# Loading raw query weights in every block, pairing the softmax sums on VectorE, turning them one step earlier, and a steeper fill rate at the end

## The chip, the cores and the metric

The kernel runs on one core of a Trainium2 chip. The metric is the device time of one execution in microseconds (us). The core's engines have names of their own in the profile: PE is TensorE (its matmuls; PEld are its weight loads), DVE is VectorE, ACT is ScalarE, POOL is GpSimd, and SP is the engine whose queue issues all of this kernel's DMAs.

## The reference

Two independent parts are computed from different inputs and laid side by side in the output. Part A is attention with 32 query heads and one shared key and value head; part B is a two-dimensional Fourier mix by matrices, of which the real part is kept.

```python
def _A_ref(x, wq, wk, wv, wo):            # x 1 x 2048 x 1024, 32 heads of 32
    q = (x @ wq).reshape(B, S, H, Dh).transpose(0, 2, 1, 3)
    k = x @ wk
    v = x @ wv
    scores = jnp.einsum("bhqd,bkd->bhqk", q, k) * (Dh ** -0.5)
    p = softmax(scores, axis=-1)
    o = jnp.einsum("bhqk,bkd->bhqd", p, v)
    return o.transpose(0, 2, 1, 3).reshape(B, S, H * Dh) @ wo

def _B_ref(x, dft_seq_re, dft_seq_im, dft_hid_re, dft_hid_im):
    a = jnp.einsum("bsd,ed->bse", x, dft_hid_re)
    b = jnp.einsum("bsd,ed->bse", x, dft_hid_im)
    return jnp.einsum("ts,bse->bte", dft_seq_re, a) - jnp.einsum("ts,bse->bte", dft_seq_im, b)

return jnp.concatenate([a, b], axis=-1)   # 1 x 2048 x 2048, all float32
```

## The kernel before

**Two streams on TensorE.** One stream is attention. It is cut into 32 units (a block `b` of 512 query rows times a group `g` of four heads), and a unit into 32 steps. The other stream is "fill": all large products that are not attention, 5664 matmuls of 512 columns. These are the projections of keys, values and queries, both stages of part B (seven products each instead of eight) and the output projection. Each float32 operand of a fill product is split into a high part and a rest (`hi`, `lo`), and three matmuls (high times high, rest times high, high times rest) make one product.

**A step of attention.** `score_step(s)` writes a 128 x 1024 piece of the scores into a PSUM tile `pss` (two matmuls), DVE takes its row maximum into `nm`, and one step later ACT takes the exponential in place, whose row sums are accumulated (`row_sums`). After the 32 steps of a unit these maxima and sums give the softmax's shift and divisor. `LSE` is a table that says in which later step `e` of the next unit each of these small operations stands: `lse_1` (DVE), `lse_1b` (an exponential on ACT), `lse_1c` (a product on POOL), `lse_2` (DVE), `lse_3` (a PE matmul with the identity that turns `nm` by 90 degrees, "the turning matmul", and a DVE copy to `mt`), `lse_4` (DMAs that put `mt` into two rows of `qst`, the query tile, and the divisors to DRAM). Twelve steps after a unit's scores end (`LEAD`), `expo(n)` begins on it: the scores once more, transposed, in a PSUM tile `pst` (two matmuls), whose exponential ACT writes to `p`. `pst` has one buffer, so the next pair of its matmuls waits for ACT. Every eighth step `pv` multiplies eight tiles `p` with `v` (128 matmuls in a unit).

**The fill's place.** Instructions stand on each engine in the order in which the Python code issues them. `pos["fill"]` counts the fill matmuls issued. `START` = 144 of them come first; up to there the splits are cast on ACT and subtracted on DVE, from there on both are on POOL. Another 66 follow, then 44 steps of scores with seven fill matmuls each (`take(7)`), and then 1024 steps of the main loop, in which `level(n)` issues as many as bring the count to a goal that rises in a straight line. In the last 44 of these steps no scores of new units are left.

**The supply of the fill.** An `Item` is one operand tile of 128 x 512. A `Line` (`RL` for the right operands `r`, `ML` for the left ones `m`) takes its items through four stages (load by DMA, combine, high part, rest), each a fixed lead ahead of the item's due place, counted in fill matmuls: 52, 36, 27 and 21 for `ML`. A raw left tile has three buffers, a split one four. An item with `pre` instead fetches both finished parts from DRAM, in `fetch`. `store` issues a DMA nine fill matmuls after the call (`BEHIND`), so it does not hold up SP's queue.

**Query weights.** `q_group(b, g, xs)` makes the query projection of one unit: 24 fill matmuls, a left operand `wq` of two items. For block 0 the items are loaded raw, split, and both parts are stored to DRAM (`wq_d`); blocks 1 to 3 fetch the two parts. The 32 query groups are the fill matmuls 96 to 864.

Of the kernel before, what the change touches and what calls it, by code (L numbers as in the profile page):

```python
# [16 lines left out]
P = 128  # L17
# [5 lines left out]
NG = 8  # L23
NQ = 4
NC = 16
# [62 lines left out]
def tile_kernel(ctx: ExitStack, tc, xT, wq, wkv, wo, xbT, wT, cT, out):  # L88
    nc = tc.nc
    te = Ordered(tc, nc.tensor)  # L90
    act = Ordered(tc, nc.scalar)
    dve = Ordered(tc, nc.vector)
    gp = Ordered(tc, nc.gpsimd)
# [13 lines left out]
    wq_d = [[[dram.tile([P, 4, P], F32, name=f"wq_{g}_{q}_{a}") for a in range(2)] for q in range(2)] for g in range(NG)]  # L107
    xr_d = [dram.tile([P, 4, P], F32, name=f"xr_{k}") for k in range(8)]
    wr_d = [[dram.tile([P, W], F32, name=f"wr_{n}_{c}") for c in range(4)] for n in range(2)]
    u_d = {(n, k): [dram.tile([P, W], F32, name=f"{k}_{n}_{s}") for s in range(8)] for n in range(2) for k in ("t", "u2", "u3", "u4")}  # L110
# [306 lines left out]
        return Group(wkv_items, xs, kv_post(b), rows=2 * DH)  # L417

    ready = set()
    seen_w = set()  # L420

    def q_group(b, g, xs):
        if g in seen_w:
            left = [Item(None, pre=lambda q=q: wq_d[g][q]) for q in range(2)]
        else:
            seen_w.add(g)
            left = [Item([(lambda q=q: wq[g, :, q * 4:(q + 1) * 4, :], 1)], save=wq_d[g][q]) for q in range(2)]

        def post(ps):
            qh = op.tile([P, W], F32R, name="qh")  # L430
            ql = op.tile([P, W], F32R, name="ql", bufs=1)
            if pos["fill"] <= START:
# [152 lines left out]
    SU = 32  # L585
    LEAD = 12
    total = SU * len(units)
    qst, nm, ls, lse, pt, ov, rb, pend = ({} for _ in range(8))
    ends = []

    def open_unit(u):
        b, g = units[u]
        assert ("q", b, g) in ready
        q = qsp.tile([P, 4, W], F32R, name="qst")
        gp.memset(q[96:P].bitcast(F32), 0.0)
        for r, src in enumerate((qh_d, ql_d, qh_d)):
            move(sp, q[r * DH:(r + 1) * DH], src[b][g].rearrange("(h d) c -> d h c", d=DH))
        qst[u] = q
        nm[u] = sm.tile([P, 6, NC], F32, name="nm")
        ls[u] = sm.tile([P, 2, NC], F32, name="ls")  # L600

    def scores(s):
        u, r = divmod(s, SU)
# [9 lines left out]
    def row_sums(s):  # L613
        if s not in pend:
            return
        ps = pend.pop(s)
        u, r = divmod(s, SU)
        i, j = divmod(r, 2)
        act.activation(ps, ps, AF.Exp, bias=nm[u][:, j, i:i + 1], accum_out=ls[u][:, j, i:i + 1])

    def over(rows):
        return rows.rearrange("p a c -> p c a")

    def lse_1(u):
        z = nm[u]
        d = sm.tile([P, 2, NC], F32, name="md")
        dve.tensor_reduce(z[:, 2], over(z[:, :2]), axis=AX.X, op=ALU.min, negate=True)
        for j in range(2):
            dve.tensor_reduce(d[:, j], over(z[:, j::2 - j][:, :2]), axis=AX.X, op=ALU.add, negate=True)
        lse[u] = d  # L630

    def lse_1b(u):
        act.activation(lse[u], lse[u], AF.Exp)

    def lse_1c(u):
        gp.tensor_mul(lse[u], lse[u], ls[u])

    def lse_2(u):
        z, d = nm[u], lse[u]
        l = sm.tile([P, NC], F32, name="l")  # L640
        dve.tensor_reduce(z[:, 3].bitcast(F32R), over(z[:, :2]), axis=AX.X, op=ALU.min)
        dve.tensor_reduce(z[:, 4], over(z[:, 2:4]), axis=AX.X, op=ALU.add, negate=True)
        dve.tensor_reduce(l, over(d), axis=AX.X, op=ALU.add)
        dve.reciprocal(z[:, 5], l)

    def lse_3(u):
        aside()
        pm = bank("psb")
        te.transpose(pm[:3 * NC, :P], nm[u][:, 3:].rearrange("p a b -> p (a b)"), ident)
# [58 lines left out]
    def score_step(s):  # L708

        if s < total:  # L710
            u, r = divmod(s, SU)
            if r == SU - 6 and u + 1 < len(units):
                open_unit(u + 1)
            scores(s)
        row_sums(s - 1)
        u, e = divmod(s - SU, SU)
        if 0 <= u < len(units):
            for f in LSE.get(e, ()):
                f(u)
# [117 lines left out]
```

## Time and profile before

| | |
|---|---|
| median of three runs | 2813.98 us (2813.29 to 2816.73) |
| the profiled execution's own time | 2816.89 us |
| its span from first to last instruction | 2815.0 us |
| PE busy | 2776.0 us, 99% of the span |
| ACT, DVE, POOL busy | 2182.6, 1612.9, 1569.4 us |
| granted TensorE clock, mean | 0.997 |
| DMA | 480.84 MB, 171 GB/s over the span |

Rows of the profile that show an instruction name its output and input tiles without their buffer numbers, then the shape, then "xN" where N equal ones are merged. A time in brackets at the end is how long the engine was idle before it, with what ended the wait. "Windows" rows give for a stretch of time its length, each engine's busy time with the number of instructions, the granted clock as a share of full speed, the busy share of the 16 DMA engines, and GB/s. A matmul's listed duration overlaps with the next one's, so the distance between the starts of two matmuls is what one costs. Nearly every instruction of the kernel stands under line 66, a helper; tiles tell them apart.

### The profile page before, as it was taken

To read this page: it belongs to the slowest core of one execution; us is meant where nothing else is said; L and a number is where in the kernel's file an instruction comes from. 1 tells how busy PE (TensorE), PEld (TensorE's weight loads), DVE (VectorE), ACT (ScalarE), POOL (GpSimd) and SP (SyncE) were. 2 spreads that over 40 slices of the span, in tenths; PEclk is the share of its full clock that TensorE was granted. 3 is DMA by queue.
4 is the path that set the end of the run, shared out by engine and by line. 5 is a ranking of instruction groups with operands and counts; after the bars stand their busy time and mean duration, and the time that the engine had idled before them with its cause. 6 is when DMAs were issued, how large, how long until landed. Compare 5 with 4: busy or idle time off the path is not lost.

```text
span 2815.0 us, 40144 instructions
## 1 busy us (share of the span) xinstructions
PE 2776.0 (99%) x13904; PEld 1935.7 (69%) x13904; DVE 1612.9 (57%) x1800; ACT 2182.6 (78%) x3151; POOL 1569.4 (56%) x1558
## 2 busy tenths in 40 slices
PE   7999999999999999999999999989999999999999
PEld 5776676767667676767666767666767676766656
DVE  5766666666666665555555555545555555555411
ACT  4578887888878788888888888878888888888740
POOL 2422233665545448767785676887888875721110
PEclk9999999999999999999999999999999999999999
DMA  8865435675576555554463454564554642545345
GB/s 292 299 199 163 156 109 169 225 231 188 195 243 211 166 178 167 152 155 142 140 191 105 127 172 122 184 198 138 183 176 146 187 139 98 159 145 145 122 143 172
DMA packets 315723, 480.84 MB, mean 171 GB/s; under 512 B 33408, under 2 KB 98432, under 8 KB 315520
## 3 DMA queue, kind: packets, MB, share of 16 engines
q1 hardware_dynamic: 315520, 478.28, 54.3%
q8 instruction: 110, 1.80, 0.3%
q14 instruction: 93, 0.76, 0.1%
HBM read 364.12 MB, written 112.98 MB: 169 GB/s over the span
## 4 chain that ended last, share of the span: by engine, by line
PE 93%; DMA 2%; POOL 1%; issue 1%; DVE 1%; SPq 1%; ACT 1%; POOLq 0%; DVEq 0%; ACTq 0%
PE psb L66 59%; PE pss L66 18%; PE pst L66 17%; DMA r<-s 1%; DMA ql<-ql 1%; SPq L66 1%; POOL ml L66 0%; DMA r<-in_xT_dram 0%; DVE nm L66 0%; POOL mh L66 0%; POOL m L66 0%; DMA wq<-mh 0%; POOL rl L66 0%; POOL rh L66 0%; POOL y L66 0%
## 5 line engine op out<-in xcount | busy, mean ns | idle before, releaser
L66 DVE TENSOR_REDUCE nm<-pss 128x1 f32<-128x1024 f32 x1024 | 1252.2, 1223 | 611.7 <-PE pss L66 610.9
L66 ACT ACTIVATE p<-pst 128x1024 f32<-128x1024 f32 x1024 | 1052.0, 1027 | 481.0 <-PE pst L66 478.9
L66 ACT ACTIVATE pss<-pss,nm 128x1024 f32<-128x1024 f32 x1024 | 1112.7, 1087 | 72.7 <-DVE nm L66 71.6
L66 PE MATMUL psb<-rh,mh 128*128 128x512 f32 (+1 forms) x1852 | 732.0, 395 | 17.9 <-ACT rh L66 8.7
L66 PE MATMUL psb<-rh,ml 128*128 128x512 f32 (+1 forms) x1852 | 731.9, 395 | 1.4 <-POOL ml L66 1.4
L66 PE MATMUL psb<-rl,mh 128*128 128x512 f32 (+1 forms) x1852 | 730.1, 394 | 0.3 <-DVE rl L66 0.3
L66 PE MATMUL pst<-qst,kst 128*128 128x512 f32 x2048 | 654.3, 400 | 5.6 <-DMA qst<-mt 4.7
L66 PE MATMUL pss<-kst,qst 128*128 128x512 f32 x2048 | 655.8, 401 | 3.2 <-ACT pss L66 3.2
L66 PEld LDWEIGHTS pss<-kst,qst 128*128 128x128 f32 x2048 | 375.6, 188 | 185.3 <-issue 100.5
L66 PE MATMUL psb<-p,v 128*32 128x512 f32 x4096 | 466.6, 596 | 0.0
L66 PEld LDWEIGHTS pst<-qst,kst 128*128 128x128 f32 x2048 | 375.8, 188 | 116.6 <-ACT p L66 26.6
L66 PEld LDWEIGHTS psb<-rh,mh 128*128 128x128 f32 (+1 forms) x1852 | 347.6, 188 | 105.8 <-ACT rh L66 10.0
L66 PEld LDWEIGHTS psb<-rh,ml 128*128 128x128 f32 (+1 forms) x1852 | 347.8, 188 | 86.0 <-POOL ml L66 2.8
L66 PEld LDWEIGHTS psb<-rl,mh 128*128 128x128 f32 (+1 forms) x1852 | 347.4, 188 | 84.2 <-DVE rl L66 1.4
L66 POOL TENSOR_TENSOR ml<-m,mh 128x512 fp32r<-128x512 f32 x292 | 376.5, 1289 | 49.2 <-ACT mh L66 43.6
L66 PEld LDWEIGHTS psb<-p,v 128*32 128x32 f32 x4096 | 120.5, 110 | 276.3 <-issue 266.0
L66 POOL TENSOR_TENSOR r<-r,r 128x512 f32<-128x512 f32 x112 | 144.3, 1288 | 269.7 <-DMA r<-in_wT_dram 135.0
L66 POOL CAST rh<-r 128x512 fp32r<-128x512 f32 x214 | 131.2, 613 | 275.0 <-PE psb L66 110.1
L66 POOL TENSOR_TENSOR rl<-r,rh 128x512 fp32r<-128x512 f32 x214 | 276.0, 1290 | 5.5
L66 POOL TENSOR_TENSOR m<-m,m 128x512 f32<-128x512 f32 x192 | 247.6, 1290 | 24.4 <-DMA m<-in_xbT_dram 18.8
L66 DVE TENSOR_TENSOR ov<-ov,psb 128x512 f32<-128x512 f32 x96 | 66.0, 687 | 314.2 <-PE psb L66 314.2
L66 POOL CAST mh<-m 128x512 fp32r<-128x512 f32 x291 | 178.0, 612 | 91.4 <-PE psb L66 76.0
(69 smaller groups left out, 926.5 us busy)
## 6 DMA issues: line engine op xcount, KB each, us to landing
m<-in_cT_dram SPq DMA_DIRECT2D x384, 256.0 KB, 3.8
r<-s SPq DMA_DIRECT2D x192, 256.0 KB, 4.4
y<-y SPq DMA_DIRECT2D x96, 256.0 KB, 4.6
r<-in_wT_dram SPq DMA_DIRECT2D x80, 256.0 KB, 3.6
m<-in_xbT_dram SPq DMA_DIRECT2D x80, 256.0 KB, 4.2
y<-u SPq DMA_DIRECT2D x80, 256.0 KB, 2.9
qst<-qh SPq DMA_DIRECT2D x64, 256.0 KB, 5.7
s<-y SPq DMA_DIRECT2D x64, 256.0 KB, 2.9
```

Source lines behind the costliest of these rows:

```text
L66: return lambda *a, **k: self.tc.keep_in_program_order(f(*a, **k))
```

## The change

1. `q_group` loads the raw weights in every block. The 32 stores to `wq_d` and the 96 fetches from it are gone; 48 loads of a raw tile, 48 casts and 48 subtractions on POOL are new.
2. The row sums are accumulated in rows 8 and 9 of `nm` (ten rows now), the exponentials of the shifts go to rows 6 and 7, and two DVE reductions with a product, in `lse_2`, take the place of `lse_1c` on POOL.
3. `lse_2` stands in step 4 instead of 6 and `lse_4` in step 8 instead of 9. `lse_3` stands in step 6 (`TURN`) in front of that step's scores, instead of in step 7 behind them.
4. The goal of `level` rises more slowly over the whole main loop, and by one more matmul a step in its last 44 steps, to the same end.

```diff
-        if g in seen_w:
-            left = [Item(None, pre=lambda q=q: wq_d[g][q]) for q in range(2)]
-        else:
-            seen_w.add(g)
-            left = [Item([(lambda q=q: wq[g, :, q * 4:(q + 1) * 4, :], 1)], save=wq_d[g][q]) for q in range(2)]
+        left = [Item([(lambda q=q: wq[g, :, q * 4:(q + 1) * 4, :], 1)]) for q in range(2)]
...
-        nm[u] = sm.tile([P, 6, NC], F32, name="nm")
-        ls[u] = sm.tile([P, 2, NC], F32, name="ls")
+        nm[u] = sm.tile([P, 10, NC], F32, name="nm")
...
-        act.activation(ps, ps, AF.Exp, bias=nm[u][:, j, i:i + 1], accum_out=ls[u][:, j, i:i + 1])
+        act.activation(ps, ps, AF.Exp, bias=nm[u][:, j, i:i + 1], accum_out=nm[u][:, 8 + j, i:i + 1])
...
-        d = sm.tile([P, 2, NC], F32, name="md")
         dve.tensor_reduce(z[:, 2], over(z[:, :2]), axis=AX.X, op=ALU.min, negate=True)
         for j in range(2):
-            dve.tensor_reduce(d[:, j], over(z[:, j::2 - j][:, :2]), axis=AX.X, op=ALU.add, negate=True)
-        lse[u] = d
+            dve.tensor_reduce(z[:, 6 + j], over(z[:, j::2 - j][:, :2]), axis=AX.X, op=ALU.add, negate=True)
 
     def lse_1b(u):
-        act.activation(lse[u], lse[u], AF.Exp)
-
-    def lse_1c(u):
-        gp.tensor_mul(lse[u], lse[u], ls[u])
+        act.activation(nm[u][:, 6:8], nm[u][:, 6:8], AF.Exp)
 
     def lse_2(u):
-        z, d = nm[u], lse[u]
+        z = nm[u]
+        d = sm.tile([P, 2, NC], F32, name="md")
         l = sm.tile([P, NC], F32, name="l")
+        for j in range(2):
+            dve.tensor_reduce(d[:, j], over(z[:, 6 + j::2][:, :2]), axis=AX.X, op=ALU.mult)
...
+        if SU <= s < SU * (len(units) + 1) and s % SU == TURN:
+            lse_3((s - SU) // SU)
+        if s < total:
             scores(s)
         row_sums(s - 1)
...
-    LSE = {1: (lse_1,), 2: (lse_1b,), 3: (lse_1c,), 6: (lse_2,), 7: (lse_3,), 9: (lse_4,)}
+    TURN = 6
+    LSE = {1: (lse_1,), 2: (lse_1b,), 4: (lse_2,), 8: (lse_4,)}
...
+    QUIET = total - SU - LEAD
+    MORE = 1
+
+    def goal(n):
+        return PRO + (FILL - PRO - LAST - MORE * (total - QUIET)) * n // total + MORE * max(n - QUIET, 0)
...
-        goal = PRO + (FILL - PRO - LAST) * (k + 1) * 8 // total
-        left = goal - pos["fill"]
+        left = goal((k + 1) * 8) - pos["fill"]
         take(left - left * (7 - r) // (8 - r))
```

Three places show what moves. The first is SP's queue while the query groups of block 0 are made, behind `START`: `m` are raw tiles of query weights, `r` tiles of the next block's x, `qh` and `ql` the two parts of a finished query group, `wq` the split weights. Before, one group's worth of the queue:

```order
L66 DMA m_949<-in_wq_dram 128x512
L66 DMA r_960<-in_xT_dram 128x512
L66 DMA wq_1_0_175<-mh 128x512
L66 DMA wq_1_1_176<-ml 128x512
L66 DMA m_980<-in_wq_dram 128x512
L66 DMA qh_2_59<-qh 128x512
L66 DMA ql_2_91<-ql 128x512
L66 DMA wq_0_0_177<-mh 128x512
L66 DMA wq_0_1_178<-ml 128x512
```

The same group's worth after the change:

```order
L66 DMA m_902<-in_wq_dram 128x512
L66 DMA r_913<-in_xT_dram 128x512
L66 DMA m_931<-in_wq_dram 128x512
L66 DMA qh_2_59<-qh 128x512
L66 DMA ql_2_91<-ql 128x512
```

Four of nine transfers are gone, and with them the waits of SP's queue for POOL's `mh` and `ml` in front of a load.

The second place is PE around the turning matmul (`psb<-ident,nm`) of unit 20, with DVE's small operations of the same unit behind it. Before, on PE:

```order
L66 MATMUL psb<-rl,mh 128x512
L66 MATMUL psb<-rh,ml 128x512
L66 MATMUL pss<-kst,qst 128x512 x2
L66 MATMUL psb<-ident,nm 48x128
L66 MATMUL pst<-qst,kst 128x512 x2
```

and after the change:

```order
L66 MATMUL psb<-rl,mh 128x512
L66 MATMUL psb<-rh,ml 128x512
L66 MATMUL psb<-ident,nm 48x128
L66 MATMUL pss<-kst,qst 128x512 x2
L66 MATMUL pst<-qst,kst 128x512 x2
```

On DVE before, from the operations of `lse_2` to the copy `mt` that waits for the turning matmul:

```order
L66 TENSOR_REDUCE nm<-nm 128x16 x2
L66 TENSOR_REDUCE l<-md 128x16
L66 RECIPROCAL nm<-l 128x16
L66 TENSOR_REDUCE nm<-pss 128x1
L66 COPY mt<-psb 48x128
```

and after the change:

```order
L66 TENSOR_REDUCE md<-nm 128x16 x2
L66 TENSOR_REDUCE nm<-nm 128x16 x2
L66 TENSOR_REDUCE l<-md 128x16
L66 RECIPROCAL nm<-l 128x16
L66 COPY h_16826<-psb 128x512
L66 TENSOR_TENSOR ov<-ov,psb 128x512
L66 TENSOR_REDUCE nm<-pss 128x1
L66 COPY mt<-psb 48x128
```

The turning matmul moved in front of its step's two `pss` matmuls and one step earlier, and `lse_2` moved two steps earlier, so that a whole step lies between the reciprocal and the matmul that reads it; the two products are new on DVE.

The third place is PE in the last 44 steps of the main loop, where a step is a pair `pst` and the fill matmuls behind it. Before, one step:

```order
L66 MATMUL pst<-qst,kst 128x512 x2
L66 MATMUL psb<-rh,mh 128x512
L66 MATMUL psb<-rl,mh 128x512
L66 MATMUL psb<-rh,ml 128x512
L66 MATMUL psb<-rh,mh 128x512
L66 MATMUL psb<-rl,mh 128x512
```

and after the change, a step at the same distance from the end:

```order
L66 MATMUL pst<-qst,kst 128x512 x2
L66 MATMUL psb<-rl,mh 128x512
L66 MATMUL psb<-rh,ml 128x512
L66 MATMUL psb<-rh,mh 128x512
L66 MATMUL psb<-rl,mh 128x512
L66 MATMUL psb<-rh,ml 128x512
L66 MATMUL psb<-rh,mh 128x512
L66 MATMUL psb<-rl,mh 128x512
```

Five or six fill matmuls stood behind a `pst` pair there, and six or seven stand there now. Counted over both programs, the 43 distances between the first `pst` pair of this stretch and the last hold 210 fill matmuls before (23 steps of five, 15 of six, five with `pv`) and 250 after (25 of six, 13 of seven, five with `pv`).

More of the change, by code (lines that the diff above doesn't have):

```diff
@@ L106, in tile_kernel @@
     r_d = [dram.tile([NC, P], F32, name=f"r_{u}") for u in range(NQ * NG)]
-    wq_d = [[[dram.tile([P, 4, P], F32, name=f"wq_{g}_{q}_{a}") for a in range(2)] for q in range(2)] for g in range(NG)]
     xr_d = [dram.tile([P, 4, P], F32, name=f"xr_{k}") for k in range(8)]
@@ L419, in tile_kernel @@
     ready = set()
-    seen_w = set()
     def q_group(b, g, xs):
-        if g in seen_w:
-            left = [Item(None, pre=lambda q=q: wq_d[g][q]) for q in range(2)]
-        else:
-            seen_w.add(g)
-            left = [Item([(lambda q=q: wq[g, :, q * 4:(q + 1) * 4, :], 1)], save=wq_d[g][q]) for q in range(2)]
+        left = [Item([(lambda q=q: wq[g, :, q * 4:(q + 1) * 4, :], 1)]) for q in range(2)]
         def post(ps):
@@ L587, in tile_kernel @@
     total = SU * len(units)
-    qst, nm, ls, lse, pt, ov, rb, pend = ({} for _ in range(8))
+    qst, nm, lse, pt, ov, rb, pend = ({} for _ in range(7))
     ends = []
@@ L648, in lse_3 @@
         pm = bank("psb")
-        te.transpose(pm[:3 * NC, :P], nm[u][:, 3:].rearrange("p a b -> p (a b)"), ident)
+        te.transpose(pm[:3 * NC, :P], nm[u][:, 3:6].rearrange("p a b -> p (a b)"), ident)
         mt = sm.tile([3 * NC, P], F32, name="mt")
```

## Prediction

> **What bounds the kernel now.** I read the page's first part, then the windows of the stretches that looked short of work, the waits, and the timeline of those stretches.
>
> ```profile
> span 2815.0 us, 40144 instructions
> PE 2776.0 (99%) x13904; PEld 1935.7 (69%) x13904; DVE 1612.9 (57%) x1800; ACT 2182.6 (78%) x3151; POOL 1569.4 (56%) x1558
> ```
>
> TensorE is the bound. The change takes no matmul away, so it can only win back time in which PE stood still or ran slowly. First, what an undisturbed stretch costs (timeline of PE in the main loop):
>
> ```profile
> 1005.77 0.62 PE L66 MATMUL pss<-kst,qst 128*128 128x512 f32 x2
> ...
> 1006.70 0.40 PE L66 MATMUL psb<-rh,mh 128*128 128x512 f32 x1
> 1006.93 0.39 PE L66 MATMUL psb<-rl,mh 128*128 128x512 f32 x1
> ...
> 1008.08 0.63 PE L66 MATMUL pss<-kst,qst 128*128 128x512 f32 x2
> ...
> 1010.17 0.63 PE L66 MATMUL pss<-kst,qst 128*128 128x512 f32 x2
> ```
>
> A matmul costs 0.23 us from start to start. A step of two `pss`, two `pst` and six fill matmuls took 2.31 us, one with five 2.09: in the main loop a fill matmul moved elsewhere is 0.23 us saved. Now the windows, in which PE does worse:
>
> ```profile
> 54.00:78.00 24.00, 16.67 (x55) 11.63 (x54) 7.39 (x9) 4.49 (x7) 16.61 (x19) 0.86 1.04 367
> 78.00:164.00 86.00, 85.17 (x368) 68.54 (x367) 64.80 (x72) 47.91 (x82) 31.55 (x33) 1.00 0.85 277
> ...
> 1850.00:1880.00 30.00, 22.63 (x88) 16.14 (x88) 12.40 (x16) 16.86 (x24) 27.13 (x28) 0.83 0.59 193
> 1880.00:1960.00 80.00, 80.00 (x411) 55.51 (x407) 46.56 (x50) 65.74 (x95) 64.56 (x63) 1.00 0.52 158
> ```
>
> From 54 to 78 us, 55 matmuls took 24 us and are worth 55 x 0.23 = 12.65: 11.3 us lost, with the DMA engines full (share 1.04). A second hole lies at 1850 us, with POOL busy 27 of 30 us. The rest of the loss is small and spread, except for a steady one at the end, below.
>
> **The start: stores that go.** DMAs issued from 44 to 80 us, and the longest wait of that time:
>
> ```profile
> q1 hardware_dynamic: 6717, 12.18, 97.5%
> m<-in_wq_dram SPq DMA_DIRECT2D x11, 256.0 KB, 5.1
> wq<-mh SPq DMA_DIRECT2D x9, 256.0 KB, 5.2
> wq<-ml SPq DMA_DIRECT2D x9, 256.0 KB, 5.2
> ...
> qst<-ql SPq DMA_DIRECT2D x1, 256.0 KB, 3.6
> ```
> ```profile
> 65.88 0.69 DVE L66 SCALAR_TENSOR_TENSOR ql<-psb,qh 128x512 fp32r<-128x512 f32 x1 [10.91 <-DMA ql<-ql]
> ```
>
> The DMA engines were 97.5% busy and a transfer took 5.2 us to land. 18 of the 45 transfers in that list's stretch store split weights. DVE stood 10.9 us because `ql` has one buffer and its store sat in that traffic; behind DVE the row maxima waited, and PE with them. POOL waited for raw weights, and PE for POOL. The change removes those 18: 12.18 MB less 18 x 0.256 is about 7.5 MB in 36 us, some 210 GB/s where 367 were moved at the worst. Bounds: nothing, if loads alone still set the pace; 11.3 us, all of it. I take 7.5: POOL needs 0.61 + 1.29 us for each weight tile (rows below) and the same for one x tile a group, 5.7 us for 24 fill matmuls that PE does in 5.5, so some waiting stays until the scores begin.
>
> What part of the 11.3 us is slow clock can be read here:
>
> ```profile
> 57.57 0.40 PE L66 MATMUL psb<-rh,ml 128*128 128x512 f32 x1
> 60.40 0.50 PE L66 MATMUL psb<-rh,mh 128*128 128x512 f32 x1 [2.43 <-POOL mh L66]
> ...
> 62.34 0.63 PE L66 MATMUL psb<-rh,mh 128*128 128x512 f32 x1
> 62.77 0.63 PE L66 MATMUL psb<-rl,mh 128*128 128x512 f32 x1
> ```
>
> After a gap of 2.83 us the matmuls ran at 0.43 us apart, 0.20 slower each, for about six: a gap of that length costs about 1.3 us more than itself. The Trainium skill ("TensorE: Matmul & The Clock Gate", What's actually happening) says that the clock halves after an idle window of about 3.4 us; by that a gap of 2.8 us would cost nothing beyond itself, the start would have 1.3 us less to win, and the sum would be 2795.4 for 2794.1. The row shows the half rate after less, and I go by the row.
>
> **The price of raw weights in blocks 1 to 3.** 48 items now pass POOL, and 96 fetches become 48 loads. POOL's prices, with those of the small products:
>
> ```profile
> L66 POOL TENSOR_TENSOR ml<-m,mh 128x512 fp32r<-128x512 f32 x292 | 376.5, 1289 | 49.2 <-ACT mh L66 43.6 <-PE psb L66 1.7
> L66 POOL CAST mh<-m 128x512 fp32r<-128x512 f32 x291 | 178.0, 612 | 91.4 <-PE psb L66 76.0 <-DMA m<-in_xbT_dram 8.7 <-DMA m<-in_wq_dram 5.3
> L66 POOL TENSOR_TENSOR md<-md,ls 128x32 f32<-128x32 f32 x32 | 8.1, 253 | 160.8 <-ACT md L66 160.0 <-PE psb L66 0.8
> L66 DVE TENSOR_REDUCE md<-nm 128x16 f32<-128x32 f32 x64 | 9.0, 183 | 1.1
> ```
>
> 48 x (0.612 + 1.289) = 91 us more of POOL, at a place where it is idle: from 78 to 164 us some 21 of the items fall due (230 fill matmuls up to the main loop, one item to 12, and the lead), 40 us on top of 31.55, 83% of 86 us. From 1880 to 1960 POOL was busy 64.56 of 80 us, 81%, and PE lost nothing. So I take zero. The cover is thinner than there: 12 fill matmuls pass in 12 / 7 steps of 2.09 us (nine matmuls), 3.6 us, and the lead of 27 is 8.1 us. If it is gone, each weight tile that comes late is PE's own wait; that is a rival below.
>
> **The pair products on DVE.** 64 x 0.183 = 11.7 us more for DVE, busy 57%, and 8.1 us less for POOL. In `lse_2` two more reductions, 0.37 us, stand in front of the next row maximum; `pss` has two buffers and a step is 2.09 us or more, so nothing on PE waits for that. What counts is that DVE no longer waits for POOL in `lse_2`.
>
> **The turning matmul.** How it fared:
>
> ```profile
> L66 PE MATMUL psb<-ident,nm 128*48 128x128 f32 x32 | 9.0, 282 | 3.4 <-DVE nm L66 2.5 <-DVE ql L66 0.8
> L66 PEld LDWEIGHTS psb<-ident,nm 128*48 128x48 f32 x32 | 3.3, 103 | 11.0 <-DVE nm L66 6.9 <-DVE ql L66 1.5 <-DVE y L66 0.9
> ```
>
> PE's lost time before the 32 turns lies between the 3.4 us of its own idle row and the 11.0 us before their weight loads, part of which runs beside a matmul. I take 5, of which 2 belong to the hole at 1850 us, counted there. In front of the scores, with `lse_2` a full step earlier, the reciprocal is long done: 3 us gained (bounds: a loss of 1, if the new place makes the `pss` weights wait; a gain of 9).
>
> **The hole at 1850 us.**
>
> ```profile
> 1855.04 0.63 PE L66 MATMUL pss<-kst,qst 128*128 128x512 f32 x2
> 1857.56 0.29 PE L66 MATMUL psb<-ident,nm 128*48 128x128 f32 x1 [1.66 <-DVE nm L66]
> ...
> 1861.76 1.05 PE L66 MATMUL pss<-kst,qst 128*128 128x512 f32 x2
> ...
> 1870.68 0.63 PE L66 MATMUL pss<-kst,qst 128*128 128x512 f32 x2
> 1876.03 1.19 PE L66 MATMUL pst<-qst,kst 128*128 128x512 f32 x2 [4.72 <-DMA qst<-mt]
> ```
> ```profile
> 1857.03 0.19 DVE L66 TENSOR_REDUCE l<-md 128x16 f32<-128x32 f32 x1 [2.12 <-POOL md L66]
> ```
> ```profile
> 1871.69 1.71 SPq L66 DMA_DIRECT2D qst<-mt  x2
> ```
>
> POOL is behind there, by the operands of two-term products. Its small product `md` came late, DVE and the turning matmul waited for it, and the step that began at 1855.04 took 6.7 us for 2.3. Then `qst<-mt` stood in SP's queue behind loads that wait for POOL until 1871.69, and `pst` started 5.35 us after `pss` for 0.46. With some slow matmuls behind each that makes about 11 us. In the changed kernel `md` does not pass POOL, `qst<-mt` is issued a step earlier, and the fill stands some 35 matmuls further back at that step (3685 for 3720 issued at unit 20's turn, counted over the programs), so that the fullest part of the stretch has not begun. The wait on `md` goes for certain, the one on `qst<-mt` most likely. POOL's lag itself stays and may hit PE through `mh` and `ml`. I take 7 gained (bounds: nothing, where another unit's turn meets the jam; 11).
>
> **The end.** Steps without scores, PE and ACT:
>
> ```profile
> 2692.32 0.67 PE L66 MATMUL pst<-qst,kst 128*128 128x512 f32 x2
> ...
> 2694.20 0.70 PE L66 MATMUL pst<-qst,kst 128*128 128x512 f32 x2
> ...
> 2697.99 0.73 PE L66 MATMUL pst<-qst,kst 128*128 128x512 f32 x2
> ...
> 2699.89 0.73 PE L66 MATMUL pst<-qst,kst 128*128 128x512 f32 x2
> ```
> ```profile
> 2698.82 1.02 ACT L66 ACTIVATE p<-pst 128x1024 f32<-128x1024 f32 x1 [0.88 <-PE pst L66]
> ```
>
> With five fill matmuls (2697.99) a step takes 1.90 us, with six (2692.32) 1.88: it is the round trip over the one `pst` buffer, 1.02 us of ACT and 0.88 back, not PE's seven matmuls, 1.6 us. The stretch holds 210 fill matmuls before and 250 after. Counted over the programs, 42 leave the main loop (40 for the stretch, one more behind it and one before the loop) and save 42 x 0.23 = 9.7 us there. In the stretch, steps of six stay at 1.9, and the 13 of seven are nine matmuls, 2.09: 13 x 0.2 = 2.6 us more; four more fill matmuls beside `pv` are 0.9, and six in place of five in the others some 0.4; the two outside cost 0.5. Net gain 9.7 - 4.4 = 5.3 (bounds 0, if the feed of the fill can't keep up, and 9.7).
>
> **The sum** on the profiled execution, 2816.89 us (1.9 around the span): 7.5 + 3 + 7 + 5.3 = 22.8 us less, 2794.1. That execution stands 2.9 us above the median of 2813.98, so on the median 2791.2. A fifth effect has no sign: every fill matmul moves against the steps by up to 42, so where a group's end meets a `pv` or a turn is drawn anew, a few waits of about 1 us.
>
> **The rivals.**
> - *The start keeps its loss*, because the raw loads' round trip sets the pace, not the traffic. For it: POOL waited for `m` there, three buffers, 5.1 us to land. Against it: 97.5% busy DMA engines with 40% of the transfers gone. Gain 1 for 7.5: 2798.
> - *The hole stays*, moved to another unit. For it: POOL's load there does not change. Against it: both waits that PE saw went through `md` or through a place in SP's queue that moves. 2798 again.
> - *POOL becomes the bound of the query groups* (slower). Three raw buffers for an item every 3.6 us: a round trip of load, cast and rest may take 10.9 us. Now it is 5.1 + 1.9 = 7.0. From 3.9 us of queueing on POOL and SP upwards each further microsecond costs 0.33 us an item; at 16 us it is 1.7 x 21 = 35 us between 78 and 164 us, and the start's gain is gone too: 2813.98 + 35 - 15 = 2834. POOL's queue holds a clearing of `qst` and an x tile in front at worst, which speaks against it.
> - *The gains do not show*: what is freed at the start is waited for at the first scores, late fill matmuls wait for their feed, and new meetings cost what the turn wins. About 2814.
>
> **How the numbers follow.** A difference under 0.2%, 5.6 us, is about what a measurement here can't tell from no change. Forecast 0.62, the first rival 0.12, the second 0.12, the third 0.06, the fourth 0.08. The first three cases are all faster: 0.86; within 0.2% 0.07 (a little of the last case falls outside); slower 0.07. The range goes from all four gains near their upper ends, some 30 us, 2783, to half of the start and of the end and little else, 2807, and takes in both rivals of 2798.
>
> **What would show it.** In the changed profile: the window from 54 to 78 us with about 85 matmuls or more, a DMA share near 0.7 and clock 1.00; no DVE wait on `ql` over 3 us; no wait of DVE for POOL in front of `l`; the turning matmuls' weight loads with under 3 us of idle time; no `pst` wait on `qst<-mt`; steps of seven fill matmuls at 2.09 us near the end, and the first step without scores about 27 us earlier on the clock (7.5 + 3 + 7 + 9.7). PE waiting on `mh` or `ml` between 78 and 164 us, or POOL at 95% there, would prove me wrong, and so would end steps of seven that take over 2.3 us.

## The result, and the profile after

The changed kernel took 2791.16 us (median of four runs, 2789.13 to 2792.41) against 2813.87 us (2813.29 to 2816.73): a ratio of 0.9917, with a 95% interval of 0.9899 to 0.9934. The forecast was 2791.2 us. The profiled execution took 2791.25 us, 25.6 us less than the one of before; the two spans are 25.7 us apart.

The page's first part of the changed kernel, then the windows that were shown of before, with the same bounds (start and end, length, busy time and count of PE, PEld, DVE, ACT and POOL, clock, DMA share, GB/s):

```profile
span 2789.3 us, 40153 instructions
PE 2763.8 (99%) x13904; PEld 1932.7 (69%) x13904; DVE 1624.4 (58%) x1864; ACT 2181.4 (78%) x3151; POOL 1651.0 (59%) x1622
```
```profile
54.00:78.00 24.00, 22.75 (x99) 18.25 (x99) 13.88 (x15) 8.63 (x15) 20.77 (x23) 1.00 0.70 237
78.00:164.00 86.00, 84.59 (x364) 67.35 (x363) 64.62 (x74) 51.18 (x85) 65.63 (x71) 1.00 0.57 188
1850.00:1880.00 30.00, 27.60 (x145) 17.47 (x146) 13.64 (x14) 19.58 (x28) 28.27 (x27) 0.94 0.58 201
```

In the 24 us from 54 on, PE now issues 99 matmuls for 55, at clock 1.00 for 0.86 and a DMA share of 0.70 for 1.04. POOL, with its 81.6 us of extra work, is at 76% from 78 to 164 us. The stretch from 1850 us is better, but not clean.

To divide the 25.7 us, three instants on PE cut the span: the first `pst` pair (the main loop begins), the first of the 44 steps without scores, and the last `pst` pair. From the timeline of PE, before and after:

```profile
164.08 0.62 PE L66 MATMUL pst<-qst,kst 128*128 128x512 f32 x2
2658.71 0.64 PE L66 MATMUL pst<-qst,kst 128*128 128x512 f32 x2
2753.36 0.73 PE L66 MATMUL pst<-qst,kst 128*128 128x512 f32 x2
```
```profile
155.87 0.62 PE L66 MATMUL pst<-qst,kst 128*128 128x512 f32 x2
2629.74 0.64 PE L66 MATMUL pst<-qst,kst 128*128 128x512 f32 x2
2727.70 0.67 PE L66 MATMUL pst<-qst,kst 128*128 128x512 f32 x2
```

| part | before | after | gain |
|---|---|---|---|
| start, to the first `pst` | 164.08 | 155.87 | 8.2 |
| main loop up to the steps without scores | 2494.63 | 2473.87 | 20.8 |
| steps without scores | 94.65 | 97.96 | -3.3 |
| behind the last `pst` | 61.6 | 61.6 | 0 |

The main loop's 20.8 us can be divided further by reading its steps one by one; a wait is taken here as the distance between the starts of two neighbouring matmuls on PE, less the usual 0.23 us. 42 fill matmuls fewer are 9.7 us. The steps of the hole (1855 to 1876 us before, 1816 to 1853 us after) were 11.6 us longer than ordinary ones and are 8.2 us longer now, a gain of 3.4. The waits in front of the turning matmuls, outside the hole, came to 2.5 us before and are 0.1 us after. One of the two largest before:

```profile
800.74 0.40 PE L66 MATMUL psb<-rh,ml 128*128 128x512 f32 x1
801.56 0.29 PE L66 MATMUL psb<-ident,nm 128*48 128x128 f32 x1 [0.42 <-DVE nm L66]
```

The last piece was not in the forecast as a gain: in the kernel before, six of the steps with a turning matmul outside the hole held a wait of 0.67 to 1.27 us on a PSUM bank, 5.9 us in all; after, one of 0.5 us is left. These four pieces make 20.9 us.

How such a wait on a bank came about, in the kernel before (timeline of DVE and PE; the turning matmul is `psb<-ident,nm`):

```profile
474.88 1.22 DVE L66 TENSOR_REDUCE nm<-pss 128x1 f32<-128x1024 f32 x1 [0.17 <-PE pss L66]
475.14 0.27 PE L66 MATMUL psb<-ident,nm 128*48 128x128 f32 x1
476.02 0.68 DVE L66 TENSOR_TENSOR y<-y,psb 128x512 f32<-128x512 f32 x1
476.75 0.50 PE L66 MATMUL psb<-rh,mh 128*128 128x512 f32 x1 [0.88 <-DVE y L66]
```

`lse_3` closes the fill group that stands in front of it (`aside()`), and DVE must then empty that group's bank (`y<-y,psb`). Behind the scores, the bank's emptying was queued on DVE after the row maximum, 1.22 us long, and PE's next group waited for the bank. After the change, the same place in the next unit, where before had such a wait too:

```profile
543.36 0.27 PE L66 MATMUL psb<-ident,nm 128*48 128x128 f32 x1
543.57 0.69 DVE L66 TENSOR_TENSOR y<-y,psb 128x512 f32<-128x512 f32 x1 [0.63 <-PE psb L66]
544.31 0.19 PEld L66 LDWEIGHTS psb<-rh,mh 128*128 128x128 f32 x1 [0.18 <-DVE y L66]
544.37 1.21 DVE L66 TENSOR_REDUCE nm<-pss 128x1 f32<-128x1024 f32 x1
```

The group ends before the scores, DVE empties its bank first and takes the row maximum second, and PE's next weight load waits 0.18 us.

### The profile page after: what moved, and what is told of

The parts are those of the page before. It is cut to its first block, busy times and chain, and to the rows that moved or that the text cites. A ratio compares the mean times of both kernels' runs of the same rounds, so it can differ in the third digit from the quotient of the medians.

```text
span 2789.3 us, 40153 instructions
## 1 busy us (share of the span) xinstructions
PE 2763.8 (99%) x13904; PEld 1932.7 (69%) x13904; DVE 1624.4 (58%) x1864; ACT 2181.4 (78%) x3151; POOL 1651.0 (59%) x1622
## 4 chain that ended last, share of the span: by engine, by line
PE 96%; DMA 1%; DVE 1%; ACT 1%; issue 0%; POOL 0%; SPq 0%; ACTq 0%; POOLq 0%; DVEq 0%
PE psb L66 61%; PE pss L66 18%; PE pst L66 17%; DMA p<-in_xT_dram 0%; DVE nm L66 0%; ACT pss L66 0%; SPq L66 0%; DVE rl L66 0%; ACT p L66 0%; DMA r<-s 0%; ACT rh L66 0%; DMA qst<-mt 0%; DMA ql<-ql 0%; DMA r<-in_xT_dram 0%; POOL ml L66 0%
## 5 line engine op out<-in xcount | busy, mean ns | idle before, releaser
L66 POOL TENSOR_TENSOR ml<-m,mh 128x512 fp32r<-128x512 f32 x340 | 438.8, 1291 | 48.2 <-ACT mh L66 40.4
L66 PEld LDWEIGHTS pst<-qst,kst 128*128 128x128 f32 x2048 | 377.4, 188 | 112.2 <-ACT p L66 20.8
L66 POOL CAST mh<-m 128x512 fp32r<-128x512 f32 x339 | 208.1, 614 | 166.0 <-PE psb L66 145.3
```

The lines of the kernel that those rows point to most:

```text
L66: return lambda *a, **k: self.tc.keep_in_program_order(f(*a, **k))
```

## The experiments

All ratios are against the kernel before, whose median was about 2814 us in every comparison. Diffs are against the changed kernel unless said otherwise.

**1. The stores of the split weights come back** (`stores_back`), in block 0 only. Nothing fetches them, so they are traffic alone.

```diff
+    wq_d = [[[dram.tile([P, 4, P], F32, ...) for a in range(2)] for q in range(2)] for g in range(NG)]
...
-        left = [Item([(lambda q=q: wq[g, :, q * 4:(q + 1) * 4, :], 1)]) for q in range(2)]
+        left = [Item([(lambda q=q: wq[g, :, q * 4:(q + 1) * 4, :], 1)], save=wq_d[g][q] if b == 0 else None) for q in range(2)]
```

> The changed kernel (2791.2 us), but block 0 stores its split weights to DRAM again (32 stores, read by nobody); blocks 1 to 3 still load raw weights. Theory A, the traffic of the stores made the hole at the start: the main loop begins about 8 us later again and the time is about 2799. Theory B, the hole came from the fetches or from the order of loads and not from the stores: about 2791 to 2793. A window from 54 to 78 us with some 55 to 65 matmuls and a full DMA share speaks for A.

2799.91 us (2796.57 to 2803.61), ratio 0.9950 (0.9937 to 0.9964): 8.75 us slower than the changed kernel. The window from 54 us, and DVE's wait on the one `ql` buffer (waits from 40 to 80 us: total, times, longest):

```profile
54.00:78.00 24.00, 18.20 (x70) 13.50 (x69) 8.81 (x10) 5.02 (x9) 17.79 (x21) 0.93 1.05 376
```
```profile
DVE ql L66 <- DMA ql<-ql: 15.0, 3, 9.2
```

With the stores alone the DMA engines are full again (1.05), DVE waits 15.0 us for `ql` (3.2 us in the same window of the changed kernel), the matmuls fall from 99 to 70, and the first `pst` comes at 162.12 us for 155.87. The start's gain is the stores' traffic.

**2. The turning matmul behind the scores again** (`turn_behind`), all else as changed.

```diff
-        if SU <= s < SU * (len(units) + 1) and s % SU == TURN:
-            lse_3((s - SU) // SU)
...
-    LSE = {1: (lse_1,), 2: (lse_1b,), 4: (lse_2,), 8: (lse_4,)}
+    LSE = {1: (lse_1,), 2: (lse_1b,), 4: (lse_2,), 6: (lse_3,), 8: (lse_4,)}
```

> The changed kernel (2791.2 us) with the turning matmul in step 6 still, but behind that step's scores; the reciprocal stays in step 4. Theory A, the place in front of the scores is what won, since four matmuls then stand between the turn and the next group's first fill matmul, so that DVE can empty the bank meanwhile: waits of about 1 us on a fresh bank come back in steps of a turn, 5 to 7 us in all, about 2797. Theory B, only the earlier reciprocal won, as the prediction had it: about 2791, a little lower if the 0.1 us that each turn costs in front of the scores goes.

2799.53 us (2795.30 to 2800.02), ratio 0.9943 (0.9931 to 0.9956): 8.4 us slower (the interval and the changed kernel's just touch). The order of before is back at the same place (timeline of DVE and PE):

```profile
543.02 1.23 DVE L66 TENSOR_REDUCE nm<-pss 128x1 f32<-128x1024 f32 x1 [0.86 <-PE pss L66]
543.04 0.27 PE L66 MATMUL psb<-ident,nm 128*48 128x128 f32 x1
544.16 0.68 DVE L66 TENSOR_TENSOR y<-y,psb 128x512 f32<-128x512 f32 x1
544.89 0.50 PE L66 MATMUL psb<-rh,mh 128*128 128x512 f32 x1 [1.10 <-DVE y L66]
```

Six such waits, of 0.68 to 1.36 us and 6.6 us in all, are back, all in turn steps. The turning matmuls themselves wait for nothing here: 0.1 us in all 32. So the place of the matmul is worth some 7 us (6.9 between the two profiled executions, 8.4 between the medians), and it is worth it through DVE's order, not through the wait of the matmul for its input.

**3. Both parts of the new order, undone** (`old_turn`): `lse_2` in step 6, `lse_3` in step 7 behind the scores, `lse_4` in step 9; the products stay on DVE.

```diff
-        if SU <= s < SU * (len(units) + 1) and s % SU == TURN:
-            lse_3((s - SU) // SU)
...
-    LSE = {1: (lse_1,), 2: (lse_1b,), 4: (lse_2,), 8: (lse_4,)}
+    LSE = {1: (lse_1,), 2: (lse_1b,), 6: (lse_2,), 7: (lse_3,), 9: (lse_4,)}
```

> The changed kernel (2791.2 us) with the whole old order of the small operations (lse_2 in step 6, the turn in step 7 behind the scores, lse_4 in step 9); pair products stay on DVE. Theory A, the new order won 6 to 7 us by itself (waits for the reciprocal and waits on a fresh bank): 2797 to 2799. Theory B, it won the 3 us of the prediction: 2794. The wait on qst<-mt near 1850 us should grow from 3.6 us by up to a step, 2 us, if its place in SP's queue matters.

2809.93 us (2806.91 to 2814.38, eleven runs), ratio 0.9985 (0.9976 to 0.9994): 18.8 us slower than the changed kernel, more than either theory. The turning matmul's weight loads (group: count, busy time, mean ns, idle time before them and what ended it), here and in the changed kernel, and PE's longest wait:

```profile
L66 PEld LDWEIGHTS psb<-ident,nm 128*48 128x48 f32 x32 | 3.3, 103 | 12.7 <-DVE nm L66 8.8 <-DVE y L66 1.3 <-DVE ql L66 1.1
...
PE pst L66 <- DMA qst<-mt: 6.8, 2, 3.6
```
```profile
L66 PEld LDWEIGHTS psb<-ident,nm 128*48 128x48 f32 x32 | 3.3, 103 | 1.3
```

The idle time before the turning loads goes from 1.3 to 12.7 us, yet PE loses only 5.0 us in front of the turning matmuls of the main loop, for 0.1, because most of that idle time lies beside a running matmul. The waits for a bank are 5.6 us again, for 0.5, and `qst<-mt`, a step later, costs a second stall of 5.5 us with its slow matmuls at 1450 us (near 1850 us its wait did not grow: 3.2 us for 3.6). Together that is 15.5 us, near the 16.3 us between the two profiled executions; the medians are 18.8 us apart, and the rest was not found in one place.

**4. The new order alone, in the kernel before** (`turn_alone`; diff against before). The product stays on POOL, in step 3.

```diff
-    LSE = {1: (lse_1,), 2: (lse_1b,), 3: (lse_1c,), 6: (lse_2,), 7: (lse_3,), 9: (lse_4,)}
+    TURN = 6
+    LSE = {1: (lse_1,), 2: (lse_1b,), 3: (lse_1c,), 4: (lse_2,), 8: (lse_4,)}
...
+        if SU <= s < SU * (len(units) + 1) and s % SU == TURN:
+            lse_3((s - SU) // SU)
```

> The kernel before (2814.0 us) with only the new order of the small operations: lse_2 in step 4, the turn in step 6 in front of the scores, lse_4 in step 8; weights, pair product on POOL and the fill's goal as before. Theory A, the place in front of the scores removes the waits on a fresh bank (seven of 0.75 to 1.45 us in turn steps, 7.7 us together) and the waits for the reciprocal, at 0.1 us a turn: 2806 to 2808, with no wait over 0.5 us on a group's first fill matmul in a turn step. Theory B, the 19 us that the old order cost in the changed kernel are its worth everywhere: about 2796. The hole near 1850 us may move, which is worth up to 5 us either way.

2813.85 us (2810.59 to 2816.72, eleven runs), ratio 0.9997 (0.9988 to 1.0006): nothing gained, which neither theory expected. Of the waits for a bank, two of 0.6 us and a new one, below, are left; but the product on POOL is now wanted two steps earlier. Timeline of DVE at the jam:

```profile
1852.92 0.19 DVE L66 TENSOR_REDUCE l<-md 128x16 f32<-128x32 f32 x1 [8.26 <-POOL md L66]
```

DVE stood 8.26 us for POOL's `md`, and everything behind it on DVE with it, the emptying of a bank included: two turning matmuls came 1.63 and 4.53 us late, and in a third unit the fill waited 3.86 us for its bank. These 10.0 us take back most of what the order could win, 5.9 us of waits for a bank and 5.3 us in front of the turning matmuls. The two profiled executions still differ by 5.7 us, since that of `turn_alone` stood 2.7 us below its median and that of before 2.9 us above; eleven runs do not bear that gain out. That the order wins only with the product off POOL is not shown by this: the next experiment puts the product back on POOL in the changed kernel and loses far less.

**5. The pair product back on POOL** (`pool_pairs`), the new order kept.

```diff
+    def lse_1c(u):
+        gp.tensor_mul(nm[u][:, 6:8], nm[u][:, 6:8], nm[u][:, 8:10])
...
-            dve.tensor_reduce(d[:, j], over(z[:, 6 + j::2][:, :2]), axis=AX.X, op=ALU.mult)
...
-    LSE = {1: (lse_1,), 2: (lse_1b,), 4: (lse_2,), 8: (lse_4,)}
+    LSE = {1: (lse_1,), 2: (lse_1b,), 3: (lse_1c,), 4: (lse_2,), 8: (lse_4,)}
```

> The changed kernel (2791.2 us) with the pair product on POOL in step 3 again, in the same rows of nm. Theory A, with the reciprocal in step 4 and the turn in step 6 a late POOL product has two steps of slack, so nothing is lost except where POOL is far behind, around 1820 to 1850 us: 2791 to 2793. Theory B, DVE waiting for POOL in front of its row maxima is what the products on DVE avoid: 2795 or more, with waits of DVE for POOL of 1 us or more in several units.

2794.23 us (2792.30 to 2797.28), ratio 0.9929 (0.9917 to 0.9942): 3.1 us slower in the medians, between the two theories, and the interval touches the changed kernel's. DVE's waits for POOL are there in seven units, each of over 1 us, as theory B has it. Only two of them reached PE, which stood idle for 4.51 and 0.77 us before the turning matmul. All the waits (total, times, longest), then the longest:

```profile
DVE l L66 <- POOL nm L66: 24.8, 7, 8.4
1836.53 0.19 DVE L66 TENSOR_REDUCE l<-nm 128x16 f32<-128x32 f32 x1 [8.40 <-POOL nm L66]
```

So most of the late products cost nothing here, and the product's move to DVE is worth about 3 us, which the intervals do not show to be more than nothing. Why the new order won nothing in `turn_alone` stays open in part: that kernel also differs from this one in the weights and in the fill's rate.

**6. The split weights fetched again** (`old_weights`): stored in block 0, fetched in blocks 1 to 3, as before.

```diff
+    wq_d = [[[dram.tile([P, 4, P], F32, ...) for a in range(2)] for q in range(2)] for g in range(NG)]
...
-        left = [Item([(lambda q=q: wq[g, :, q * 4:(q + 1) * 4, :], 1)]) for q in range(2)]
+        if b:
+            left = [Item(None, pre=lambda q=q: wq_d[g][q]) for q in range(2)]
+        else:
+            left = [Item([(lambda q=q: wq[g, :, q * 4:(q + 1) * 4, :], 1)], save=wq_d[g][q]) for q in range(2)]
```

> The changed kernel (2791.2 us) with the old weights in full: block 0 stores both parts, blocks 1 to 3 fetch them. Theory A, the stores alone made the hole and POOL's extra 91 us cost nothing: as with the stores alone, about 2799. Theory B, the raw weights in blocks 1 to 3 cost something on POOL that the start's gain hides: below 2797, that is faster than the kernel with stores and raw weights. Theory C, the fetches add to the traffic: above 2800.

2802.43 us (2800.60 to 2803.26), ratio 0.9958 (0.9944 to 0.9972). That is 11.3 us slower than the changed kernel. It is 2.5 us slower than the stores alone in the medians, but the intervals overlap, so theory C, which its number fits, isn't shown against theory A. The start is that of the stores:

```profile
54.00:78.00 24.00, 16.85 (x65) 12.48 (x64) 7.29 (x8) 4.35 (x7) 16.34 (x18) 0.93 1.05 375
```

With the 91 us of splitting gone from POOL no time was won. A cost of that work could hide here only behind an equal cost of the fetches, and the changed kernel's waits show none.

**7. and 8. Other fill rates at the end** (`more0`, `more2`): the edit is `MORE = 0` or `MORE = 2` for `MORE = 1`.

> The changed kernel (2791.2 us) with the old straight goal of the fill (MORE = 0). Theory A, the fill moved to the end is worth what the step costs say (42 x 0.23 us in the main loop less 3.3 us at the end and 0.5 elsewhere, 5.9): about 2797, with the last 43 distances between pst pairs 94.6 us long for 98.0. Theory B, the main loop's shorter time came from elsewhere: about 2791 to 2793.

> The changed kernel (2791.2 us) with MORE = 2: another 40 or so fill matmuls from the main loop to the last 44 steps. Theory A, steps of six still have 0.02 to 0.2 us of slack by the round trip over pst and steps of seven have none: the main loop wins 9.6 us, the end gives back about 8 to 9: 2790 to 2791. Theory B, the end's steps have more slack than that: 2787 or less. Theory C, the fill's feed can't keep up there: 2794 or more, with PE waiting on mh or rh.

2792.77 us (2792.11 to 2795.38, ratio 0.9925, 0.9913 to 0.9937) and 2793.99 us (2791.24 to 2795.21, ratio 0.9926, 0.9914 to 0.9939). First and last `pst` of the stretch without scores, with 0 and with 2:

```profile
2634.16 0.64 PE L66 MATMUL pst<-qst,kst 128*128 128x512 f32 x2
2728.86 0.74 PE L66 MATMUL pst<-qst,kst 128*128 128x512 f32 x2
```
```profile
2623.68 0.64 PE L66 MATMUL pst<-qst,kst 128*128 128x512 f32 x2
2729.05 0.62 PE L66 MATMUL pst<-qst,kst 128*128 128x512 f32 x2
```

The stretch takes 94.7, 98.0 and 105.4 us with 0, 1 and 2: the first 40 fill matmuls moved in cost 3.3 us there, the next ones 7.4. The main loop gives back 6.4 us for the first (2480.2 for 2473.9, in an execution whose hole, with the waits behind it, was 2.9 us milder; 9.3 us without that, for the 9.7 of 42 x 0.23; whether the old rate itself makes the hole milder is open) and 7.3 for the second, nothing net. As a total the term is too small for these measurements: the three intervals overlap. With 0, the median lies only 1.6 us above the changed kernel's, in the range of theory B and not in that of theory A; with 2, it lies above theory A's range, near theory C's, but PE nowhere waits for `mh` or `rh` in that stretch, as theory C would have it.

**9. `qst<-mt` on another queue** (`act_queue`), ACT's instead of SP's, to take it from behind the loads that wait for POOL.

```diff
-            move(sp, qst[u][96 + a:97 + a].rearrange("o h (t c) -> o (h t) c", c=P), mt[a * NC:(a + 1) * NC])
+            move(act, qst[u][96 + a:97 + a].rearrange("o h (t c) -> o (h t) c", c=P), mt[a * NC:(a + 1) * NC])
```

> The changed kernel (2791.2 us) with the two DMAs qst<-mt of each unit issued on ACT's queue instead of SP's. Theory A, the 3.6 us that pst waits for qst<-mt near 1850 us come from the loads ahead of it in SP's queue, which wait for POOL: the wait goes with the slow matmuls behind it, 5 us, and the issue on ACT costs little: about 2787. Theory B, ACT's issue (about 1 us a unit) delays its exponentials and PE with them by 0.2 to 1 us a unit: 2792 to 2810. Theory C, POOL's lag is the limit there and PE waits for mh or ml instead: about 2790.

2846.00 us (2845.26 to 2850.74), ratio 1.0117 (1.0103 to 1.0130): far worse than any of the theories. Timeline of ACT, then its waits over the whole span:

```profile
1355.28 0.52 ACTq L66 DMA_DIRECT2D qst<-mt  x1
1361.44 0.52 ACTq L66 DMA_DIRECT2D qst<-mt  x1
1362.00 1.02 ACT L66 ACTIVATE p<-pst 128x1024 f32<-128x1024 f32 x1 [5.66 <-DMA m<-in_cT_dram]
```
```profile
ACT p L66 <- DMA m<-in_cT_dram: 24.0, 4, 6.4
ACT p L66 <- DMA y<-y: 22.6, 3, 11.5
```

Between the two DMAs of a pair, 6.16 us passed, and by the profile what ended the wait was the landing of a load that SP had issued and that these DMAs have nothing to do with. ACT's exponentials stood behind it, and PE behind them. These two rows of ACT's waits come to 46.6 us, beside the 54.8 us that the kernel lost.

**10. to 12. Trying to close the hole at 1850 us.** `lse4_early` moves `lse_4`, and with it `qst<-mt`, a step earlier (`7: (lse_4,)` for 8). `dve_y` takes 16 of POOL's additions in part B's second stage to DVE. `one_y_early` does the first, and gives one of two additions of that stage to DVE.

```diff
-        for mt, nt, outs in PRODUCTS:
+        for at_, (mt, nt, outs) in enumerate(PRODUCTS):
+            ye = dve if at_ == 3 else gp
...
-                                (gp.tensor_add if sg > 0 else gp.tensor_sub)(it.y, it.y, h)
+                                (ye.tensor_add if sg > 0 else ye.tensor_sub)(it.y, it.y, h)
```

(`dve_y`; in `one_y_early` the loop over the two outputs reads `for ye, (sg, it, to) in zip((ye, gp), plan)`.)

> The changed kernel (2791.2 us) with the 16 additions of partial outputs of the fourth product of stage 2 (the one with two-term left operands and two outputs) on DVE instead of POOL. Theory A, POOL's load is the cause of the hole near 1850 us: 16 x 1.29 = 20.6 us less for POOL in some 100 us take it away, 7 to 8 us: about 2784, with POOL near 75% busy from 1780 to 1850 us and no wait of pst on qst<-mt over 1 us. Theory B, the DMA queue's own order is the cause and POOL's load only stands beside it: 2790 to 2792. Theory C, two DVE operations of 0.69 us more per group delay the row maxima: above 2793.

> The changed kernel (2791.2 us) with lse_4 in step 7 instead of 8, so that qst<-mt stands a step earlier in SP's queue. Theory A, its place in that queue sets the wait of 3.6 us near 1850 us: it shrinks by the loads that no longer stand in front, 2 to 4 us: 2787 to 2789. Theory B, POOL's lag is the limit, and what pst does not wait the fill waits for on ml: 2790 to 2791. Theory C, SP now waits for mt itself in every unit and holds the loads behind it: above 2793.

> The changed kernel (2791.2 us) with lse_4 in step 7 (2788.6 us by itself), and of the two partial outputs of each group of the fourth product of stage 2 one is added on DVE and one on POOL. Theory A, POOL's lag is what PE waits for there (6 us of waits on ml with lse_4 in step 7), and one DVE operation of 0.69 us a group still fits beside the row maxima: 10 us less for POOL take most of it: 2783 to 2786, with PE's waits on ml from 1770 to 1885 us under 2 us. Theory B, any DVE operation more at a group's end delays the row maxima, as both did (2794): 2788 to 2791, with waits on ACT's pss in their place.

| kernel | median, us | ratio | interval |
|---|---|---|---|
| `dve_y` | 2794.44 (2792.16 to 2796.56) | 0.9928 | 0.9916 to 0.9941 |
| `lse4_early` | 2788.60 (2787.20 to 2790.67) | 0.9908 | 0.9895 to 0.9922 |
| `one_y_early` | 2787.98 (2785.05 to 2792.34) | 0.9908 | 0.9895 to 0.9922 |

PE's waits from 1770 to 1885 us: two lines of the changed kernel, then `lse4_early`, `dve_y` and `one_y_early`:

```profile
PE pst L66 <- DMA qst<-mt: 3.6, 1, 3.6
PE psb L66 <- POOL ml L66: 2.2, 3, 1.0
```
```profile
PE psb L66 <- POOL ml L66: 6.0, 4, 2.6
```
```profile
PE pss L66 <- ACT pss L66: 4.1, 5, 1.5
PE pst L66 <- DMA qst<-mt: 1.6, 1, 1.6
```
```profile
PE psb L66 <- POOL ml L66: 3.9, 3, 1.4
```

By its time, `dve_y` came out as its theory C has it, `lse4_early` as its theory A and `one_y_early` as its theory B; the waits tell more. The wait is handed on. Issued a step earlier, `qst<-mt` is no longer waited for, and PE then waits 6.0 us for POOL's `ml` where it had waited 2.2: POOL's lag had run on behind the stall. With the additions on DVE, POOL keeps up, and row maxima come late instead, with ACT's exponentials behind them. What those additions cost on DVE (group of `dve_y`), beside an operation of DVE on two SBUF tiles of the same size in the kernel before, the single one of its kind, at the end:

```profile
L66 DVE TENSOR_TENSOR y<-y,h 128x512 f32<-128x512 f32 x16 | 18.4, 1188 | 0.3
```
```profile
L66 DVE TENSOR_TENSOR ov<-ov,rb 128x512 f32<-128x512 f32 x1 | 0.7, 691 | 0.0
```

With half of the additions moved and `qst<-mt` early, 2787.98 us, no better than the early DMA alone within these measurements. Both beat the kernel before; that they beat the changed kernel, by 2.6 and 3.2 us in the medians, is likely and not shown, as the intervals overlap.

## Why the prediction was right, and where its parts were not

The forecast of 2791.2 us met 2791.16, but that it met it so closely is luck. One term was 3.6 us too large, a gain of 5.4 us was not in the sum, and the profiled executions lie 25.7 us apart for the 22.8 forecast. The medians lie 22.7 us apart, because the execution of before that was profiled stood 2.9 us above its median. On the profiled executions:

| term | forecast gain | measured |
|---|---|---|
| start | 7.5 | 8.2, with the first unit's turn in it |
| turning matmul, its waits outside the hole | 3 | 2.4, and the 1.0 in the start |
| waits for a bank in turn steps | "no sign" | 5.4 |
| hole at 1850 us | 7 | 3.4 |
| end: 9.7 less 4.4 | 5.3 | 9.7 - 3.3 = 6.4 |
| POOL's 91 us, DVE's 11.7 us | 0 | 0 |
| not placed | | -0.1 |

**The start held, by its own reason.** The traffic of the stores was the cause (experiment 1), the gain is 8.2 us for 7.5, and the rival by which the raw loads' round trip sets the pace falls. "No DVE wait on `ql` over 3 us" came true: three waits, 3.8 us in all, the longest 1.8. One term was open to chance: in executions with the same code up to there, the first `pst` came between 153.9 and 157.2 us, so the start's gain is known to about 2 us.

**The turn's waits held; the larger gain beside them was missed.** In front of the 32 turning matmuls PE lost 5.3 us before: 1.0 in the start, 1.8 in the hole, 2.5 elsewhere. After, it lost 0.1, and the weight loads' idle time is 1.3 us, as forecast. So "I take 5, of which 2 belong to the hole" was well sized, though its bounds were wide. What the sum lacked is what the new place won besides, and it lay in the sentence "a fifth effect has no sign". It has one: DVE's order at the end of a fill group is a matter of the instruction order, not of chance. Before, it stood against PE in each of the seven units (one of them in the hole) whose group ended behind the scores of the turn's step, while the two units whose group ended ahead of them show no such wait. `turn_behind` separates the two gains: there no turning matmul waits, and the waits for a bank are back. The timeline of one turn step on DVE as well as on PE would have shown it; I had read the turn's wait and not its neighbour's. (The counts 3685 and 3720 that the prediction gives for "unit 20" are those of the next unit, 21 counted from 0, whose turn before meets the hole.)

**The hole was over-sized.** "The wait on `md` goes for certain" held. Before, the group of `l` had 2.7 us of waits for POOL's `md`; after:

```profile
L66 DVE TENSOR_REDUCE l<-md 128x16 f32<-128x32 f32 x32 | 5.7, 177 | 0.0
```

"The one on `qst<-mt` most likely" failed, and with it "no `pst` wait on `qst<-mt`". SP's queue and PE in the changed kernel, with the queue's wait between 1838 and 1850 us:

```profile
1840.99 0.43 SPq L66 DMA_DIRECT2D out_dram<-y  x1
1845.49 0.81 SPq L66 DMA_DIRECT2D m<-in_cT_dram  x2
...
1847.35 1.14 SPq L66 DMA_DIRECT2D qst<-mt  x2
...
1852.40 1.19 PE L66 MATMUL pst<-qst,kst 128*128 128x512 f32 x2 [3.60 <-DMA qst<-mt]
```
```profile
SPq L66 <- POOL ml L66: 8.0, 2, 4.0
```

One step earlier, the DMA still stood behind a load that waited 4 us for POOL. In `lse4_early` it stands ahead of that load and is issued at 1841.11: one step more was needed. That run also points to POOL and not to the queue as the source of the jam, so the forecast's own sentence, "POOL's lag itself stays and may hit PE through `mh` and `ml`", was the right one, and I priced it too low. The rival by which the hole stays was half right: 3.4 of the 7 us came.

**The end held in the profile, and is not shown as a total.** Steps of seven fill matmuls took 2.08 us (two neighbouring ones of the changed kernel):

```profile
2682.77 0.62 PE L66 MATMUL pst<-qst,kst 128*128 128x512 f32 x2
2684.85 0.62 PE L66 MATMUL pst<-qst,kst 128*128 128x512 f32 x2
```

The stretch grew by 3.3 us for the 3.9 allowed, and the first step without scores came 29.0 us earlier for 27. `more2` shows where the cover ends: the next 40 cost their full price. But the kernel without this part (`more0`) is only 1.6 us slower in the medians, so what the part is worth in the whole, 5.3 us or less, stays open.

**POOL's extra work cost nothing**, as taken: 76% busy from 78 to 164 us for 83% forecast, no wait of PE for `mh` or `ml` in that window, and `old_weights`, without the work, was no faster. The rival that made POOL the bound of the query groups falls.

**The slow clock.** After the idle time of 3.60 us that the row of PE at 1852.40 us shows, the `pst` pair took 1.19 us for 0.63, and the window's granted clock was 0.94. The Trainium skill ("TensorE: Matmul & The Clock Gate", What's actually happening) speaks of an idle window of about 3.4 us, which this wait fits. Below that length the runs show both outcomes. The idle time of 2.43 us that the prediction quotes from the start of before was followed by slow matmuls, but only behind a second wait of 0.46 us, at 61.75 us, that its extract leaves out. In `lse4_early`, the matmul at 1867.77 us came after 2.65 us of idle time, and those behind it stood 0.34 us and then the usual 0.22 to 0.24 us apart. So the prediction's 1.3 us of extra cost for a gap of that length is no rule.

## What to carry to other kernels

Where two engines exchange buffers, the order on the engine that empties them decides: a short instruction placed so that a group ends before the long instruction of its emptier, not behind it, was worth some 7 us here. An operation moved earlier asks for its inputs earlier: in the kernel before, the same move alone made POOL's product late and won nothing. And where an engine lags for a stretch, removing one wait on it hands time to the next, so price the lag, not the wait.

## What the runs showed of the hardware that was not expected

- With DMAs on ACT's queue, ACT's arithmetic stood up to 11.5 us, by the profile until the landing of a transfer that SP had issued (`act_queue`). That the two queues share something by which landings are counted is inferred from the releasers that the waits name; it was not tried apart.
- DVE's additions of two SBUF tiles took 1188 ns on average in `dve_y`, 691 to 1784 ns each; the two of them during which POOL was busy for less than half of the time took 691 and 693 ns. In the kernel before, the 38 subtractions of two SBUF tiles at its start, where POOL had nothing to do, took 670 to 694 ns. Additions with one PSUM input took 687 ns on average, spread over the whole of before:

```profile
L66 DVE TENSOR_TENSOR ov<-ov,psb 128x512 f32<-128x512 f32 x96 | 66.0, 687 | 314.2 <-PE psb L66 314.2
```

  The Trainium skill ("GPSIMD Engine Reference", 1. Specifications) names contention of GpSimd with DVE instructions that have two SBUF inputs; these times agree.
